# Loading K and V through a DRAM view with 32 KB rows, in an attention forward-and-backward kernel for one core

## The chip, the cores and the metric

One core of one Trainium2 chip. Times are device microseconds of that core.

PE is the engine of matrix products, DVE that of vectors, ACT that of activations. SP (SyncE) issues loads here and POOL (GpSimd) stores. A DMA moves data between DRAM and SBUF, the memory that the engines work on; 16 DMA engines do it. A descriptor is one run of bytes that a copy reads or writes in one piece, and a packet is one record of a DMA engine in the trace.

## The reference, cut to what matters

One token attends to a cache of 4,096 positions with 32 heads of 128, beside a small dense layer. The function returns the output and the gradients of all inputs.

```python
q = (x @ wq).reshape(B, Sq, H, Dh).transpose(0, 2, 1, 3)          # H = 32, Dh = 128
scores = einsum("bhqd,bhkd->bhqk", q, k_cache) * Dh ** -0.5       # Sk = 4096
p = softmax(scores)
o = einsum("bhqk,bhkd->bhqd", p, v_cache)
a = o.transpose(...).reshape(B, Sq, H * Dh) @ wo
# out = g * a + (1 - g) * b ; then the vjp: dK and dV are as large as K and V
```

K and V are 1 MB a head each and are read once. dK and dV are 1 MB a head each and are written once. That is 134 of the 165 MB that the kernel moves. The weights and their gradients are the rest.

## The kernel before

A tile of K has partition p holding positions 32p to 32p+31, so 8 KB in one run in each partition. In DRAM the runs of neighbouring partitions also follow each other: four partitions are 32 KB in one run. That is what the change wants to use.

```python
Kv = A_k_cache.rearrange("b h (p j) d -> (b h) p j d", p=P)     # P = 128, j = 32
Vv = A_v_cache.rearrange("b h (p j) d -> (b h) p j d", p=P)
# ... four buffers each of Kn and Vn, five of dV/dK, three of wo_g, four of the transposed tiles:
outs = ctx.enter_context(tc.tile_pool(name="outs", bufs=5))
tsb = ctx.enter_context(tc.tile_pool(name="tsb", bufs=4))

def load_k(h):
    if h < H:
        kts[h] = kv_in.tile([P, J, Dh], BF16, name="Kn", tag="Kn", bufs=KB)
        nc.sync.dma_start(kts[h][:], Kv[h])
# ... load_v the same with Vn and Vv
def load_wo(g):
    if g < NG:
        wos[g] = wts.tile([P, G, D], BF16, name="wo_g", tag="wo_g", bufs=3)
        nc.sync.dma_start(wos[g][:], wo_v[g])
# ... the main loop; all loads go through the one SP queue, in this order
for h in range(H):
    hh, g = h % G, h // G
    if hh == 3:
        load_wo(g + 2)          # waits until the store of dwo has left this wo_g buffer
        # ... load_wq every other time
    load_k(h + 3)
    load_v(h + 3)
    # ... steps of the projections
    period(h)                   # transposes, softmax, dP, dQ; dK and dV on VectorE
    # dK and dV are stored by nc.gpsimd.dma_start, the POOL queue
```

Of the kernel before, what the change touches and what calls it, by code (L numbers as in the profile page):

```python
# [16 lines left out]
def kernel(  # L17
# [24 lines left out]
    nc = tc.nc  # L42
    P = 128
# [18 lines left out]
    assert Dh == P and J % 8 == 0 and D % P == 0 and H % WG == 0  # L62
    assert 0 < FR <= P and FCN == 14

    Kv = A_k_cache.rearrange("b h (p j) d -> (b h) p j d", p=P)
    Vv = A_v_cache.rearrange("b h (p j) d -> (b h) p j d", p=P)
    dKv = out_2.rearrange("b h (p j) d -> (b h) p j d", p=P)
    dVv = out_3.rearrange("b h (p j) d -> (b h) p j d", p=P)
    wq_v = A_wq.rearrange("(rc r) c -> r rc c", r=P)
# [43 lines left out]
    kts, vts, wqs, wos = {}, {}, {}, {}  # L113

    def load_k(h):
        if h < H:
            kts[h] = kv_in.tile([P, J, Dh], BF16, name="Kn", tag="Kn", bufs=KB)
            nc.sync.dma_start(kts[h][:], Kv[h])

    def load_v(h):  # L120
        if h < H:
            vts[h] = kv_in.tile([P, J, Dh], BF16, name="Vn", tag="Vn", bufs=VB)
            nc.sync.dma_start(vts[h][:], Vv[h])

    def load_wq(w):
        if w < H // WG:
# [15 lines left out]
    load_wq(0)  # L142
    load_wo(0)
    load_k(0)
    load_v(0)
    load_k(1)
    load_v(1)
    load_wo(1)
    w1_sb = mlp.tile([P, RC, F], BF16, name="w1_sb", tag="w1_sb")
# [3 lines left out]
    nc.sync.dma_start(b1c[:, 0:FM], b1_v)  # L153
    nc.sync.dma_start(b1c[0:FR, FM:FCN], B_b1[FB:F].rearrange("(p c) -> p c", c=1))
    load_k(2)
    load_v(2)
    load_w2(0)
    w2r = mlp.tile([FR, D], BF16, name="w2r", tag="w2r")
# [688 lines left out]
```

## Time and profile before

| what | before |
|---|---|
| time, median of 3 runs | 413.23 us (413.08 to 413.69) |
| span of the profiled run | 411.8 us |
| SP load queue (q1), POOL store queue (q0), of 16 engines' span | 48.3%, 48.2% |
| DVE, PE, ACT busy | 74%, 72%, 43% |

These are lines of the page of before. The first two are the span in 40 equal slices: the busy tenths of the 16 DMA engines, and the GB/s they moved. The next two are the DMA queues: packets, MB, share of 16 engines' span. The last four are the DMA issues: how many, KB each, and the median us from issue to landing.

```profile
DMA  7999999999999999999999999999999999999990
GB/s 293 419 416 400 424 423 415 424 422 423 421 425 422 423 418 421 423 423 420 424 420 423 423 407 420 421 406 386 399 421 419 426 419 422 422 384 372 377 358 14
...
q1 hardware_dynamic: 14404, 82.03, 48.3%
q0 software_dynamic: 12240, 82.03, 48.2%
...
Kn<-in_A_k_cache_dram SPq DMA_DIRECT2D x32, 1024.0 KB, 23.9
Vn<-in_A_v_cache_dram SPq DMA_DIRECT2D x32, 1024.0 KB, 29.0
out_dram<-dV_sb POOLq DMA_DIRECT2D x32, 1024.0 KB, 11.8
out_dram<-dK_sb POOLq DMA_DIRECT2D x31, 1024.0 KB, 12.0
```

The digit is 9 from the second slice to the last but one, at 415 to 426 GB/s in most slices (29 of 40).

The chain that ended last, as the page of before has it (first by engine, then by line):

```profile
DMA 38%; DVE 33%; PE 19%; ACT 4%; issue 3%; POOL 0%; ACTq 0%; SPq 0%; POOLq 0%; DVEq 0%
DMA Kn<-in_A_k_cache_dram 30%; PE tr L586 8%; DVE dK_sb L611 7%; DVE dV_sb L611 7%; DMA out_dram<-dV_sb 6%; DVE junk L382 4%; ACT tT L588 3%; PE sA L655 3%; DVE junk L285 3%; PE sA L595 2%; PE sB L708 2%; DVE junk L534 1%; DVE junk L491 1%; DMA vec_rows<-in_gate_w_dram 1%; DVE dj L695 1%
```

Who waited for whom in before (us in total, times, longest), two lines of it:

```profile
PE tr L586 <- DMA Kn<-in_A_k_cache_dram: 6.5, 4, 2.3
...
DVE dK_sb L611 <- DMA out_dram<-dV_sb: 4.4, 1, 4.4
```

```profile
SPq L133 <- DMA out_dram<-wo_g: 54.1, 5, 14.1
```

Waiting for K is 30% of the chain, yet PE waits for it 6.5 us in all. The table by stretches shows where the DMA is not full. The last two columns are the DMA share and the GB/s, and a full DMA reads 1.01 or so:

```profile
core 0: us, PE busy (x) PEld busy (x) DVE busy (x) ACT busy (x) POOL busy (x), PEclk, DMA share, GB/s
220.00:260.00 40.00, 34.57 (x646) 31.53 (x647) 35.21 (x87) 23.00 (x51) 5.92 (x11) 0.93 1.01 417
360.00:370.00 10.00, 4.40 (x73) 3.84 (x69) 5.61 (x14) 3.07 (x7) 1.36 (x2) 0.94 0.95 396
370.00:380.00 10.00, 9.17 (x146) 8.64 (x145) 7.19 (x15) 4.09 (x9) 3.81 (x5) 0.72 0.89 359
380.00:390.00 10.00, 4.34 (x119) 3.57 (x117) 9.05 (x18) 1.79 (x6) 4.30 (x6) 0.79 0.94 376
360.00:390.00 30.00, 17.91 (x331) 16.05 (x327) 21.85 (x44) 8.95 (x21) 9.46 (x13) 0.82 0.93 377
```

### The profile page before, as it was taken

How to read it: one execution, taken by the hardware profiler on the slowest of the kernel's cores; microseconds unless marked ns; L12 is line 12 of the kernel's file. 1: busy time of each engine (PE TensorE's matmuls, PEld its weight loads, DVE VectorE, ACT ScalarE, POOL GpSimd, SP SyncE). 2: the span in 40 equal slices, each digit the busy share in tenths (PEclk: the TensorE clock that was granted, in tenths of full speed). 3: DMA queues.
4: the chain of work that ended last, by engine and by line, in shares of the span. 5: the costliest groups of instructions: out<-in, count | busy, mean ns of one | idle time of the engine just before them, and what ended most of it. 6: DMA issues, size and time to landing. Idle time of an engine off the chain costs nothing.

```text
span 411.8 us, 13602 instructions
## 1 busy us (share of the span) xinstructions
PE 296.3 (72%) x5872; PEld 268.2 (65%) x5872; DVE 303.1 (74%) x791; ACT 177.1 (43%) x411; POOL 50.8 (12%) x99
## 2 busy tenths in 40 slices
PE   0688898588887888188887888338887789949300
PEld 0578787587786777178877777338777778848200
DVE  3339666856899999377698898537999997957860
ACT  1355555254545555046542557215554455534000
POOL 0001111000111111011101112001111121113410
PEclk9999999889999999779996999758999999997755
DMA  7999999999999999999999999999999999999990
GB/s 293 419 416 400 424 423 415 424 422 423 421 425 422 423 418 421 423 423 420 424 420 423 423 407 420 421 406 386 399 421 419 426 419 422 422 384 372 377 358 14
DMA packets 26744, 164.93 MB, mean 401 GB/s; under 512 B 2956, under 2 KB 3020, under 8 KB 10428
## 3 DMA queue, kind: packets, MB, share of 16 engines
q1 hardware_dynamic: 14404, 82.03, 48.3%
q0 software_dynamic: 12240, 82.03, 48.2%
q8 instruction: 46, 0.75, 0.7%
q14 instruction: 14, 0.11, 0.1%
q10 hardware_dynamic: 40, 0.01, 0.0%
HBM read 82.03 MB, written 82.03 MB: 398 GB/s over the span
## 4 chain that ended last, share of the span: by engine, by line
DMA 38%; DVE 33%; PE 19%; ACT 4%; issue 3%; POOL 0%; ACTq 0%; SPq 0%; POOLq 0%; DVEq 0%
DMA Kn<-in_A_k_cache_dram 30%; PE tr L586 8%; DVE dK_sb L611 7%; DVE dV_sb L611 7%; DMA out_dram<-dV_sb 6%; DVE junk L382 4%; ACT tT L588 3%; PE sA L655 3%; DVE junk L285 3%; PE sA L595 2%; PE sB L708 2%; DVE junk L534 1%; DVE junk L491 1%; DMA vec_rows<-in_gate_w_dram 1%; DVE dj L695 1%
## 5 line engine op out<-in xcount | busy, mean ns | idle before, releaser
L588 ACT COPY tT<-tr 128x512 f32<-128x512 f32 x256 | 142.2, 587 | 129.7 <-PE tr L586 128.9
L595 PEld LDWEIGHTS <-tT 128*128 128x128 bf16 x2048 | 79.7, 98 | 44.4 <-ACT tT L588 34.5
L586 PE MATMUL tr<-ident_f,Kn 128*128 128x128 f32 x512 | 82.2, 299 | 6.5 <-DMA Kn<-in_A_k_cache_dram 6.5
L611 DVE TENSOR_TENSOR dK_sb<-ds_bf,qd 128x2048 bf16<-128x2048 bf16 x64 | 77.7, 1215 | 4.4 <-DMA out_dram<-dV_sb 4.4
L611 DVE TENSOR_TENSOR dV_sb<-p_bf,qd 128x2048 bf16<-128x2048 bf16 x64 | 77.9, 1218 | 0.2 <-issue 0.2
L586 PE MATMUL tr<-ident_f,Vn 128*128 128x128 f32 x512 | 72.5, 277 | 0.0
L586 PEld LDWEIGHTS tr<-ident_f,Kn 128*128 128x128 f32 x512 | 61.6, 153 | 7.7 <-issue 5.2
L595 PE MATMUL sA<-qd,tT 128*128 128x48 bf16 x1024 | 48.6, 187 | 23.7 <-ACT dq_all L713 12.8
L586 PEld LDWEIGHTS tr<-ident_f,Vn 128*128 128x128 f32 x512 | 55.9, 141 | 0.0
L595 PE MATMUL sB<-qd,tT 128*128 128x48 bf16 x1024 | 46.3, 183 | 0.0
L638 POOL DMA_DIRECT2D out_dram<-dV_sb x32 | 18.2, 569 | 170.2 <-DVE dV_sb L611 58.5
L655 PEld LDWEIGHTS <-Vn 128*128 128x128 bf16 x1024 | 30.6, 96 | 10.4 <-issue 10.4
L655 PE MATMUL sA<-e_bf,Vn 128*128 128x48 bf16 x1024 | 31.2, 184 | 7.6 <-DVE zs L675 6.2
L628 POOL DMA_DIRECT2D out_dram<-dK_sb x31 | 18.3, 591 | 145.3 <-DVE rz L677 97.2
L708 PE MATMUL sB<-ds_bf,Kn 128*128 128x48 bf16 x1024 | 31.5, 184 | 1.4 <-DVE ds_bf L697 1.4
L708 PEld LDWEIGHTS <-Kn 128*128 128x128 bf16 x1024 | 28.9, 97 | 1.6 <-issue 1.6
L659 DVE TENSOR_REDUCE m<-sA 128x1 f32<-128x32 f32 x32 | 6.0, 189 | 32.2 <-PE sA L595 25.6
L285 DVE SCALAR_TENSOR_TENSOR junk<-wo_g,da_bc 128x640 bf16<-128x640 bf16 x32 | 26.2, 820 | 1.7 <-ACT da_bc L226 1.1
L695 DVE TENSOR_SCALAR_CACHE_REDUCE dj<-sB,rz 128x128 f32<-128x128 f32 x32 | 11.1, 345 | 21.3 <-PE sB L689 21.3
L382 DVE SCALAR_TENSOR_TENSOR junk<-wq_g,dq_bc 128x1024 bf16<-128x1024 bf16 (+1 forms) x25 | 25.1, 1005 | 0.2
L275 PE MATMUL qc_ps<-cols_bf,wq_g 128*128 128x1 bf16 x160 | 5.3, 164 | 22.1 <-DMA wq_g<-in_A_wq_dram 22.1
L275 PEld LDWEIGHTS <-wq_g 128*128 128x128 bf16 x160 | 4.8, 100 | 22.6 <-DMA wq_g<-in_A_wq_dram 22.4
(154 smaller groups left out, 280.7 us busy)
## 6 DMA issues: line engine op xcount, KB each, us to landing
Kn<-in_A_k_cache_dram SPq DMA_DIRECT2D x32, 1024.0 KB, 23.9
Vn<-in_A_v_cache_dram SPq DMA_DIRECT2D x32, 1024.0 KB, 29.0
out_dram<-dV_sb POOLq DMA_DIRECT2D x32, 1024.0 KB, 11.8
out_dram<-dK_sb POOLq DMA_DIRECT2D x31, 1024.0 KB, 12.0
wq_g<-in_A_wq_dram SPq DMA_DIRECT2D x4, 1280.0 KB, 30.3
wo_g<-in_A_wo_dram SPq DMA_DIRECT2D x8, 640.0 KB, 7.4
out_dram<-wo_g POOLq DMA_DIRECT2D x8, 640.0 KB, 11.3
out_dram<-dwq_t POOLq DMA_DIRECT2D x5, 896.0 KB, 14.4
```

The lines of the kernel that those rows point to most:

```text
L275: nc.tensor.matmul(qc_ps[:, hh:hh + 1], lhsT=wq[:, rc, off + hh * Dh:off + (hh + 1) * Dh], rhs=x_bf[:, rc:rc + 1], start=(rc == 0), stop=( ...
L285: nc.vector.scalar_tensor_tensor(junk[:, 0:D], in0=wos[g][:, i, :], scalar=1.0, in1=da_bc[:], op0=ALU.mult, op1=ALU.mult, accum_out=gp["do ...
L382: nc.vector.scalar_tensor_tensor(junk[:, c0:c1], in0=wqs[w][:, rc, c0:c1], scalar=1.0, in1=dq_bc[:, w * WG * Dh + c0:w * WG * Dh + c1], op ...
L586: nc.tensor.transpose(tp[:, t, :], flat[:, k * P:(k + 1) * P], ident_f[:])
L588: nc.scalar.copy(sb[:].rearrange("p a b -> p (a b)"), tp[:].rearrange("p a b -> p (a b)"))
L595: nc.tensor.matmul(out[:, 2 * k:2 * k + W], lhsT=tb[:, t, par, :], rhs=vec[:, par, :].unsqueeze(1).to_broadcast([P, W // 2, 2]), start=(pa ...
L611: nc.vector.tensor_tensor(dst[:, a:b, :].rearrange("p j (a b) -> p j a b", b=2), col[:, a:b, :].unsqueeze(2).to_broadcast([P, n, Dh // 2, 2]),
L628: nc.gpsimd.dma_start(dKv[h], st["dK"][:])
L638: nc.gpsimd.dma_start(dVv[h], st["dV"][:])
L655: nc.tensor.matmul(O, lhsT=vts[h][:, j, :], rhs=st["e"][:, j:j + 1].to_broadcast([P, W]), start=(j == 0), stop=(j == J - 1))
L695: nc.vector.tensor_scalar(dj[:], PT, rz[:], None, ALU.mult, ALU.add, accum_out=dd[:])
L708: nc.tensor.matmul(DQ, lhsT=kts[h][:, j, :], rhs=ds[:, j, 0:1].to_broadcast([P, W]), start=(j == 0), stop=(j == J - 1))
```

## The change

Its intent: let one read descriptor cover the 32 KB of four partitions, so that a quarter as many packets carry K and V, while the writes into SBUF stay 8 KB each.

```diff
-    Kv = A_k_cache.rearrange("b h (p j) d -> (b h) p j d", p=P)
-    Vv = A_v_cache.rearrange("b h (p j) d -> (b h) p j d", p=P)
+    Kw = A_k_cache.rearrange("b h (c r) d -> (b h) c (r d)", c=P // 4)
+    Vw = A_v_cache.rearrange("b h (c r) d -> (b h) c (r d)", c=P // 4)
# ... in load_k and load_v
-            nc.sync.dma_start(kts[h][:], Kv[h])
+            nc.sync.dma_start(kts[h][:].rearrange("p j d -> p (j d)"), Kw[h])
-            nc.sync.dma_start(vts[h][:], Vv[h])
+            nc.sync.dma_start(vts[h][:].rearrange("p j d -> p (j d)"), Vw[h])
```

## The prediction

> **What bounds the kernel now.** The 16 DMA engines. The page's 40 slices show DMA busy at "9" from the second slice to the last but one, about 420 GB/s. The queue table gives the SP load queue 48.3% and the POOL store queue 48.2% of 16 engines' span, 82 MB each: with instruction fetch 97% of 411.8 us. No compute engine is near that (DVE 74%, PE 72%). In the chain of waits K loads are the largest entry (30%, four stretches of 27 to 34 us), yet the waits view has PE waiting for K only 6.5 us in all: progress, freeing of buffers and issue of loads go round together at the speed of the DMA. The table by stretches shows where the engines are not full: DMA share 0.79 in the first 10 us, 0.95, 0.89 and 0.94 in 360 to 390 us (1.01 to 1.02 when full), then a drain to about 401 us and 10 us of end work.
>
> **What the change does.** Bytes, issues, buffers and compute stay. The reads of K and V change: 8,192 descriptors of 8 KB become 2,048 of 32 KB, for 67 of the 165 MB moved. The 8 KB writes into SBUF stay. Two effects:
>
> 1. Cost per packet. The packet records fit a line: 2,048 B took 84 ns, 5,120 B 196, 8,192 B 309: 0.0366 ns per byte and 9 ns fixed.[...] If it goes with the read packet, 32 KB takes about 1,209 ns (estimate from that line) instead of 4 x 309 = 1,236: 27 ns times 128 packets per engine, 3.5 us. If the writes set it, nothing. I count half: 1.7 us, all critical, since the DMA is full.
>
> 2. Arbitration.[...] from about 50 to 70 us each queue gets half. With load packets four times as large, a backlogged load queue should get about four fifths. Loads then land much sooner (now 23.9 us for K, 29.0 for V, median), stores later (now 11.8) while loads are queued, and PE's waits for K turn into DVE waits for the five output buffers (4.4 us now). As the DMA is full either way, this moves work and saves little: the thin stretch at 360 to 390 us, about 2.5 us of idle DMA, fills, because the last loads land earlier and more stores are left. I count 1.5 us.
>
> **Prediction.** 413.2 - 3.2 = 410.0 us, within 404 to 417 (8 in 10). Faster by over 2% 0.10, within 2% 0.80, slower by over 2% 0.10.
>
> **What would show it.** Step 1: load packets of 32,768 B at about 1,209 ns, and some 6,100 packets fewer. Step 2: median K and V landing under 20 us, dV and dK landing longer, new DVE waits for stores at the outer products, DMA share in 360 to 390 us near 1.01. Unchanged: compute durations, bytes, DMA share about 97%.
>
> **What would make it wrong.**[...] If starved stores stop DVE, and through it PE, while the load queue has nothing to do, gaps appear in the DMA row. If the gaps I don't count (start, 250 to 300 us) also fill, 406 is possible.

The sum: 1.7 + 1.5 = 3.2 us. The 9 ns come from the line through the packet times of before, and that they go with the read, by half, was the guess. The four fifths are the estimate: in before two queues with packets of 8 KB share the bytes by halves (4.22 MB of loads, 4.18 of stores from 50 to 70 us); if packets four times as large came as often as those of the other queue, they would have four of five bytes. The trace of before does not show that; wide16, wide32 and both2 below test it.

## More of the kernel before

Executions of the kernel before all lay between 412.89 and 413.93 us (0.3%).

The dwo gradient is computed into its own wo_g buffer and stored from there, so this buffer comes free when the store has landed.

## The result, and the profile after

The changed kernel took 413.17 us (median of 4 runs, 412.91 to 413.59) against 413.27 us of before in the same rounds (413.08 to 413.69). The ratio is 0.9997, 95% interval 0.998 to 1.0015: the same. (A ratio is the mean time of one kernel's runs over that of the other's of the same rounds, so it is not quite the ratio of the medians.) Executions over 1.5% slower than the fastest of the same kernel are left out of the means.

The same lines of the page of after:

```profile
DMA  7999999999999999999999999999999999999980
GB/s 290 418 415 404 422 424 414 422 423 422 421 424 423 421 423 415 425 423 424 421 420 424 423 407 419 422 416 390 414 421 424 422 422 421 422 379 383 401 338 14
...
q1 hardware_dynamic: 14404, 82.03, 48.5%
q0 software_dynamic: 12240, 82.03, 48.1%
...
Kn<-in_A_k_cache_dram SPq DMA_DIRECT2D x32, 1024.0 KB, 23.3
Vn<-in_A_v_cache_dram SPq DMA_DIRECT2D x32, 1024.0 KB, 28.9
out_dram<-dV_sb POOLq DMA_DIRECT2D x32, 1024.0 KB, 11.6
out_dram<-dK_sb POOLq DMA_DIRECT2D x31, 1024.0 KB, 12.7
```

The packet counts are what they were, to the packet: 14,404 on the load queue. A quarter as many K and V packets would have left 8,260. Loads land after 23.3 and 28.9 us, as before, and stores after about 12 us. None of the signs that the prediction named is there.

The chain of after, and the waits that answer to those of before:

```profile
DVE 36%; DMA 33%; PE 17%; issue 6%; ACT 4%; POOL 1%; ACTq 0%; SPq 0%; POOLq 0%; DVEq 0%
DMA Kn<-in_A_k_cache_dram 23%; DVE dK_sb L611 9%; DVE dV_sb L611 8%; PE tr L586 7%; DMA out_dram<-dV_sb 6%; DVE junk L382 4%; ACT tT L588 3%; PE sA L655 3%; DMA out_dram<-wo_g 3%; DVE junk L285 3%; PE sA L595 2%; PE sB L708 2%; DVE junk L534 1%; DVE junk L491 1%; DMA vec_rows<-in_gate_w_dram 1%
```

```profile
PE tr L586 <- DMA Kn<-in_A_k_cache_dram: 6.1, 4, 2.2
...
DVE dK_sb L611 <- DMA out_dram<-dV_sb: 4.6, 1, 4.6
```

```profile
SPq L133 <- DMA out_dram<-wo_g: 53.6, 5, 13.5
```

K has 23% of the chain instead of 30%, while the waits are the same within half a us. The chain follows whichever of several near-equal waits came last, so its shares differ between two executions that do the same work. The stretches of after, with the columns of before (so too in all tables of stretches below):

```profile
220.00:260.00 40.00, 34.74 (x637) 31.73 (x638) 35.14 (x88) 22.57 (x51) 5.94 (x11) 0.92 1.01 418
360.00:370.00 10.00, 4.52 (x78) 4.08 (x79) 5.35 (x10) 2.94 (x8) 1.84 (x2) 0.83 0.89 374
370.00:380.00 10.00, 9.04 (x164) 8.31 (x162) 7.73 (x17) 5.00 (x11) 3.30 (x6) 0.83 0.96 389
380.00:390.00 10.00, 3.21 (x85) 2.50 (x80) 8.84 (x21) 0.54 (x3) 3.86 (x6) 0.68 1.00 400
```

The stretches near the end differ too: 0.89, 0.96, 1.00 instead of 0.95, 0.89, 0.94, and 0.95 instead of 0.93 over the 30 us. The program turned out to be the same (next paragraph), so this is the size of the difference between two executions. The prediction had read 1.5 us of gain from such lines.

**The program.** The two kernels were built and their instructions compared, field by field. Every instruction, wait and buffer is equal; only the recorded source text differs. This is the load of K for head 0, in both:

```
opcode DMACopy, queue qSPDynamicHW
read  in_A_k_cache_dram  [step 4096, count 128] [step 1, count 4096]   (elements of 2 bytes)
write Kn                 [step 4096, count 128] [step 1, count 4096]
```

As written in the changed kernel the read side is [step 16384, count 32] [step 1, count 16384]. In the finished program both sides have the shorter run, that of the write: the builder has turned 32 rows of 32 KB into 128 rows of 8 KB again. So the change never reached the chip. In the program of wide32 below, whose loads are issued by hand, 31 loads of K do have [step 16384, count 32].

### The profile page after: what moved, and what is told of

Same layout as the page of the kernel before. It is cut to its first block, busy times and chain, and to the rows that moved or that the text cites. A ratio compares the mean times of both kernels' runs of the same rounds, so it can differ in the third digit from the quotient of the medians.

```text
span 410.8 us, 13602 instructions
## 1 busy us (share of the span) xinstructions
PE 298.9 (73%) x5872; PEld 270.8 (66%) x5872; DVE 303.1 (74%) x791; ACT 177.3 (43%) x411; POOL 50.9 (12%) x99
## 3 DMA queue, kind: packets, MB, share of 16 engines
q1 hardware_dynamic: 14404, 82.03, 48.5%
## 4 chain that ended last, share of the span: by engine, by line
DVE 36%; DMA 33%; PE 17%; issue 6%; ACT 4%; POOL 1%; ACTq 0%; SPq 0%; POOLq 0%; DVEq 0%
DMA Kn<-in_A_k_cache_dram 23%; DVE dK_sb L611 9%; DVE dV_sb L611 8%; PE tr L586 7%; DMA out_dram<-dV_sb 6%; DVE junk L382 4%; ACT tT L588 3%; PE sA L655 3%; DMA out_dram<-wo_g 3%; DVE junk L285 3%; PE sA L595 2%; PE sB L708 2%; DVE junk L534 1%; DVE junk L491 1%; DMA vec_rows<-in_gate_w_dram 1%
## 5 line engine op out<-in xcount | busy, mean ns | idle before, releaser
L586 PE MATMUL tr<-ident_f,Kn 128*128 128x128 f32 x512 | 84.2, 304 | 6.1 <-DMA Kn<-in_A_k_cache_dram 6.1
L611 DVE TENSOR_TENSOR dK_sb<-ds_bf,qd 128x2048 bf16<-128x2048 bf16 x64 | 77.7, 1215 | 4.6 <-DMA out_dram<-dV_sb 4.6
L611 DVE TENSOR_TENSOR dV_sb<-p_bf,qd 128x2048 bf16<-128x2048 bf16 x64 | 78.0, 1218 | 0.3 <-issue 0.3
L586 PEld LDWEIGHTS tr<-ident_f,Kn 128*128 128x128 f32 x512 | 63.2, 156 | 7.3 <-issue 6.2
L638 POOL DMA_DIRECT2D out_dram<-dV_sb x32 | 18.3, 571 | 167.8 <-DVE dV_sb L611 57.1
L628 POOL DMA_DIRECT2D out_dram<-dK_sb x31 | 18.3, 592 | 146.1 <-DVE rz L677 96.8
L275 PE MATMUL qc_ps<-cols_bf,wq_g 128*128 128x1 bf16 x160 | 5.4, 164 | 19.8 <-DMA wq_g<-in_A_wq_dram 19.5
L275 PEld LDWEIGHTS <-wq_g 128*128 128x128 bf16 x160 | 4.9, 99 | 20.4 <-DMA wq_g<-in_A_wq_dram 19.8
## 6 DMA issues: line engine op xcount, KB each, us to landing
Kn<-in_A_k_cache_dram SPq DMA_DIRECT2D x32, 1024.0 KB, 23.3
Vn<-in_A_v_cache_dram SPq DMA_DIRECT2D x32, 1024.0 KB, 28.9
```

Of the source, the lines that this page charges most:

```text
L275: nc.tensor.matmul(qc_ps[:, hh:hh + 1], lhsT=wq[:, rc, off + hh * Dh:off + (hh + 1) * Dh], rhs=x_bf[:, rc:rc + 1], start=(rc == 0), stop=( ...
L586: nc.tensor.transpose(tp[:, t, :], flat[:, k * P:(k + 1) * P], ident_f[:])
L611: nc.vector.tensor_tensor(dst[:, a:b, :].rearrange("p j (a b) -> p j a b", b=2), col[:, a:b, :].unsqueeze(2).to_broadcast([P, n, Dh // 2, 2]),
L628: nc.gpsimd.dma_start(dKv[h], st["dK"][:])
L638: nc.gpsimd.dma_start(dVv[h], st["dV"][:])
```

## The experiments

Theory A: the change had no effect because the program is the same, and real 32 KB reads do what the prediction said of them (or something else, to be seen). Rival B: the chip did read 32 KB at a time, the records list only the 8 KB writes, and the size of a read matters to nothing. The comparison of the programs speaks for A. It does not show what a record of a wide read looks like, nor whether the prediction's two effects exist. For that the loads were issued by hand, so that the two sides stay in the program as written. All runs gave correct results.

| run | reads, writes of K and V | other edit | median us | before in the same rounds | ratio (95%) |
|---|---|---|---|---|---|
| plain8 | 8 KB, 8 KB | by hand | 413.51 | 413.32 | 1.0002 (0.999 to 1.0015) |
| wide32 | 32 KB, 8 KB | by hand | 415.55 | 413.32 | 1.0045 (1.0031 to 1.0058) |
| write2 | 8 KB, 2 KB | by hand | 421.57 | 413.32 | 1.0199 (1.0185 to 1.0213) |
| both2 | 2 KB, 2 KB | by hand | 425.73 | 413.32 | 1.0295 (1.0278 to 1.0311) |
| wide16 | 16 KB, 8 KB | by hand | 413.60 | 413.42 | 1.0006 (0.9993 to 1.0019) |
| plain_late | 8 KB, 8 KB | wo after K, V | 414.75 | 413.42 | 1.0039 (1.0026 to 1.0052) |
| wide32_late | 32 KB, 8 KB | wo after K, V | 415.77 | 413.42 | 1.0048 (1.0036 to 1.006) |
| wide16_late | 16 KB, 8 KB | wo after K, V | 414.50 | 413.42 | 1.0027 (1.0014 to 1.004) |
| tail32 | 32 KB from head 27 on | by hand | 413.68 | 413.33 | 1.0007 (0.9995 to 1.0019) |
| early32 | 32 KB in heads 1 to 26 | by hand | 414.98 | 413.33 | 1.0046 (1.0029 to 1.0063) |
| plain_wo4 | 8 KB, 8 KB | four wo_g buffers | 413.62 | 413.51 | 1.0002 (0.9988 to 1.0016) |
| wide32_wo4 | 32 KB, 8 KB | four wo_g buffers | 414.68 | 413.51 | 1.0029 (1.0016 to 1.0042) |

By a measure of 2%, only both2 is slower, write2 is unclear (its interval holds 1.02) and all others are the same as before. Below, "slower" is said where the interval of the ratio leaves out 1; most of these differences are half a per cent or less.

### plain8: the hand-built load, with nothing changed

Head 0 is loaded as before in all hand-built kernels: a first build without that did not compile.

```diff
+    def load_as(h, out, in_, out_p, in_p):
+        if h == 0:
+            nc.sync.dma_start(out_p, in_p)
+            return
+        src = copy.replace(nc.sync.lower_ap_dma(in_)[0], is_dma=False)
+        dst = copy.replace(nc.sync.lower_ap_dma(out)[0], is_dma=False)
+        nc.sync.add_instruction(mybir.InstDMACopy(
+            name=nc.get_next_instruction_name(), engine=mybir.EngineType.SP, ins=[src], outs=[dst],
+            mode="Copy", queue="qSPDynamicHW", cce_op=ALU.bypass))
+    Kw = A_k_cache.rearrange("b h (c r) d -> (b h) c (r d)", c=Sk * Dh * 2 // 8192)
# ... Vw the same
-            nc.sync.dma_start(kts[h][:], Kv[h])
+            load_as(h, kts[h][:].rearrange("p j d -> p (j d)"), Kw[h], kts[h][:], Kv[h])
# ... V the same
```

> Control: the K and V loads of heads 1 to 31 built by hand, 8 KB read and 8 KB write descriptors as before. Both theories: same time as before within 0.5% (412 to 415 us), 8,192 load packets of 8,192 B at 309 ns, K and V landing at 23 to 29 us. Only the SP issue of each load may get a few tenths of a us longer.

Measured: 413.51 us, ratio 1.0002, 8,192 packets of 8,192 B. The way the load is issued costs nothing that these runs resolve.

### wide32: reads of 32 KB, for real

```diff
-    Kw = A_k_cache.rearrange("b h (c r) d -> (b h) c (r d)", c=Sk * Dh * 2 // 8192)
+    Kw = A_k_cache.rearrange("b h (c r) d -> (b h) c (r d)", c=Sk * Dh * 2 // 32768)
```

> The read descriptors of heads 1 to 31 really are 32 KB, writes 8 KB. Theory A (the change never reached the program, since the builder matched the two sides to 8 KB again): this run differs in the trace from the change: about 1,984 load packets of 32,768 B in the records instead of 7,936 of 8,192 B, and the two effects of the prediction appear: 1,209 to 1,236 ns a packet, K and V landing under 20 us, new DVE waits for stores; time 408 to 413 us. Rival B (the change did issue 32 KB reads, but records list the 8 KB writes and the size of reads matters to nothing): trace and time as those of the change, 413 us, 8,192 B packets, K landing 23 us. Rival C:[...] packets well over 1,236 ns and over 417 us.

Measured: 415.55 us, ratio 1.0045. The ratio stands for 1.9 us more than before, the medians for 2.2; the profiled execution was the slowest of the five (416.66 us). Lines of its page, the load queue and the issues:

```profile
q1 hardware_dynamic: 8452, 82.03, 48.2%
...
Kn<-in_A_k_cache_dram SPq DMA_DIRECT2D x32, 1024.0 KB, 18.3
Vn<-in_A_v_cache_dram SPq DMA_DIRECT2D x32, 1024.0 KB, 19.5
out_dram<-dV_sb POOLq DMA_DIRECT2D x32, 1024.0 KB, 19.8
out_dram<-dK_sb POOLq DMA_DIRECT2D x31, 1024.0 KB, 19.4
```

The load queue has 8,452 packets, and the packet records list 1,984 of 32,768 B. So a record is a read, rival B falls, and the changed kernel, whose trace has none of these, did not read 32 KB at a time. Rival C, whose assumed cause is cut above as no run shows it, falls as well: the packets are not well over 1,236 ns (mean 1,241), and the time is not over 417 us.

The prediction's second effect is there: K and V land sooner (18.3 and 19.5 us instead of 23.9 and 29.0), stores later (19.8 and 19.4 instead of 11.8 and 12.0). The waits of DVE for output buffers grew from 4.4 to 21.2 us, and SP's wait for wo_g buffers from 54.1 to 87.6 us. (The helper moves the line numbers by 14: L625 is before's L611.)

```profile
DVE dV_sb L625 <- DMA out_dram<-dK_sb: 11.0, 3, 4.8
...
DVE dK_sb L625 <- DMA out_dram<-dV_sb: 10.2, 3, 8.1
```

```profile
SPq L147 <- DMA out_dram<-wo_g: 87.6, 5, 19.1
```

The stretches:

```profile
220.00:260.00 40.00, 31.69 (x609) 29.02 (x609) 34.90 (x87) 18.35 (x43) 5.36 (x10) 0.85 0.95 363
240.00:250.00 10.00, 8.30 (x165) 7.39 (x166) 9.60 (x25) 5.37 (x13) 1.07 (x2) 1.00 0.84 343
360.00:390.00 30.00, 21.93 (x453) 19.76 (x450) 26.23 (x56) 12.44 (x29) 8.38 (x11) 0.92 0.98 401
```

From 220 to 260 us the DMA share is 0.95 instead of 1.01, and 0.84 from 240 to 250 us. SP issues nothing between 233 and 250 us in this run: it stands at the load of wo, whose buffer waits for a starved store (15.3 us from issue to landing), and the loads of K and V stand behind it. From 360 to 390 us the share is up, 0.98 instead of 0.93, as the prediction had it. But the kernel is slower.

The packet records give the first effect (mean times of packets; "fastest" is the lowest 1%):

| run | K and V packet | forecast by the line | fastest | median | mean | sum of K and V, over 16 engines |
|---|---|---|---|---|---|---|
| before | 8,192 B | 309 | 309 | 309 | 312.4 | 160.0 us |
| wide16 | 16,384 B | 609 | 611 | 612 | 616.2 | 157.8 us |
| wide32 | 32,768 B | 1,209 | 1,213 | 1,231 | 1,241.2 | 158.9 us |
| wide32_wo4 | 32,768 B | 1,209 | 1,213 | 1,229 | 1,254.7 | 160.6 us |

The fastest packets nearly meet the line: 1,213 ns against 4 x 309 = 1,236, so 7.7 ns for each read saved. On average, 32 KB packets take longer than the line has it, for a reason that no run here shows. The sum of K and V is 2.2 us less than before in wide16, just what the line gives, 1.1 us less in wide32 and not less at all in wide32_wo4; the four runs with the reads and the order of loads of before (before, after, plain8, plain_wo4) have 159.9 to 160.1. In wide16 and wide32 the 2,048 B packets of the other loads grew, from a mean of 87.9 ns to 94.4 and 95.8 (87.9 to 89.8 in those four). The 5,120 B ones went from 204.2 to 214.0 in wide32, but to 215.3 in plain8 as well, so that is scatter. All packets together took 402.4 us over 16 engines in wide32, against 401.0 in before and 400.2 to 401.3 in those four. The saving of step 1 is real packet by packet, and neither this sum nor the time shows it. (The sum is not the time either: in both2 it grows by 20.6 us and the time by 12.4.)

### write2 and both2: where the fixed cost of a packet sits

```diff
# write2: reads 8 KB, writes 2 KB
+    Kw = A_k_cache.rearrange("b h (p s r) d -> (b h) p s (r d)", p=P, s=1)
+            load_as(h, kts[h][:].rearrange("p (s r) d -> p s (r d)", s=4), Kw[h], kts[h][:], Kv[h])
# both2: s=4 on both sides
```

(The reverse, reads of 2 KB and writes of 8 KB, did not compile.)

> Reads stay 8 KB, writes are 2 KB. If the fixed 9 ns goes with the read packet (prediction, step 1): load packets stay 8,192 B at 309 ns and the time stays at 413 us. If it goes with the write descriptor: four times 84 = 336 ns for 8 KB, 27 ns times 496 per engine, 13.4 us more, 427 us.

> Reads and writes both 2 KB. The line of packet times gives 84 ns per 2 KB, 336 ns for 8 KB instead of 309: 13.4 us more, about 427 us. Arbitration by packets: against 8 KB stores the loads get about a fifth while both queues are backlogged, so stores land sooner than the 11.8 us of before (under 9 us) and PE waits for K grow over 6.5 us. If engines share by bytes or time instead, landings stay near those of before plus a few per cent.

Measured: write2 421.57 us, neither 413 nor 427. Its load packets are still 8,192 B, with a mean of 323.8 ns instead of 312.4, so on average 3.8 ns for each of the three added writes; store packets grew from 314.4 to 319.9 ns as well. The fastest 1% still took 309 ns, so this is not a cost that every packet pays. But the time is 8.2 us longer: more writes cost time with the reads unchanged. That is why counting half of step 1 was not foolish; but the half that belongs to reads did not show up in the time when reads got larger.

both2 took 425.73 us, 12.4 us more than before (425.73 - 413.32), near the 13.4 expected. Of these, 8.2 came with the shorter writes (write2) and 4.2 more with the shorter reads (425.73 - 421.57). PE's waits for K grew to 22.9 us and stores landed after 8.8 us, as expected.

The shares of the two queues also come out near the forecast, but only in short slices. Over stretches of 5 us the median share of the load queue in the bytes of both2 is about 0.5, because bursts of stores alternate with loads alone. So the traces were cut into slices of 0.5 us, and those kept in which nearly all traffic of each queue (97%) was K and V, or dK and dV. In before, the load queue's share lies between 0.4 and 0.6 in 189 of 297 slices. With reads of 16 KB it lies between 0.6 and 0.8 in 173 of 302 (wide16), with 32 KB between 0.7 and 0.9 in 136 of 259 (wide32). With 2 KB it lies between 0.1 and 0.3 in 198 of 371, and over 0.8, where hardly a store is left, in 66. One record of each queue in turn would give 0.50, 0.67, 0.80 and 0.20. So in most of these slices the shares fit turns that go by records, whatever their size, and not by bytes, which would give 0.50 in all four. How many records make up one turn, no run here shows.

### plain_late and wide32_late: wo after K and V

```diff
     if hh == 3:
-        load_wo(g + 2)
# ...
     load_k(h + 3)
     load_v(h + 3)
+    if hh == 3:
+        load_wo(g + 2)
```

> Control, 8 KB reads: the load of wo for group g+2 is put after K and V of the same head on the SP queue instead of ahead of them. In before SP waits 54 us for the wo_g buffers, but its load queue does not run dry meanwhile, so both theories expect no gain: 412 to 414 us.

> Real 32 KB reads (415.6 us) with the same reordering. Theory A: the loss in wide32 is the SP queue held up by the wait for a wo_g buffer (87.6 us), whose store is starved, while K and V queue up behind it and the load queue runs dry (DMA share 0.78 to 0.89 at 240 to 250 us). Then that dip goes, and the time falls to 410 to 413 us. Rival B: the loss is DVE waiting for output buffers (21 us of waits for stores): then the dip stays and the time stays at 414.5 to 416.5 us. Rival C: the packets themselves are slower than the line gives (mean 1,241 ns instead of 1,209): then the dip goes but the time stays over 413.5 us.

Measured: plain_late 414.75 us, slower than before by 0.4%, which I had not expected: DVE now waits 32.4 us for the late wo itself. wide32_late 415.77 us. The dip from 240 to 250 us is gone (DMA share 1.03 instead of 0.84), and SP's waits for wo_g stores fell from 87.6 to 46.0 us, but the time did not fall. That is what rival C expected. But the edit costs something of its own, so the pair does not settle the question; against its control wide32_late is 1.0 us slower by the medians (415.77 - 414.75), and the two intervals overlap.

### wide16 and wide16_late: half the width

The edits are those of wide32 and wide32_late with 16384 in place of 32768.

> Reads of 16 KB. Split by packet size: while both queues are backlogged the loads get about two thirds or a little less (32 KB got about three quarters, 8 KB half). Landing of K and V between 19 and 28 us, of stores between 12 and 19 us. Time between before and wide32: 412 to 415 us; packets of 16,384 B at 609 to 620 ns.

> Reads of 16 KB with wo after K and V. Theory A: 410.5 to 413 us, at or under the control; rivals: no better than wide16.

Measured: wide16 413.60 us, the same as before (ratio 1.0006). Landing lies between: K 19.4, V 24.0, dV 17.1 us. DVE waits for stores 11.2 us. All packets together took 400.7 us over 16 engines against 401.0. The line would have saved 2.2 us here (one read in two, 9 ns, 248 packets per engine), and the packets of K and V alone did save that (157.8 against 160.0). wide16_late 414.50 us, no better than its control within 0.1%.

### tail32 and early32: the end and the rest apart

```diff
-        if h == 0:
+        if h < 27:                  # tail32
+        if h == 0 or h >= 27:       # early32
             nc.sync.dma_start(out_p, in_p)
```

The load of head 27 is issued when head 24 begins, after the last load of wo. So tail32 has what step 2 counted on, without the queue held up by wo.

> 32 KB reads only for the loads of heads 27 to 31, which are issued after the last load of wo, so that nothing on the SP queue waits for a starved store. Theory A (wide32 gains at the end what the prediction counted in step 2, and loses more in the middle): DMA share at 360 to 390 us over 0.96 on average instead of 0.93, no dip at 220 to 260 us, time 411.5 to 412.8 us. Rival B (wide reads bring nothing anywhere, the end included): 413.2 to 414.5 us.

> The complement: 32 KB reads for heads 1 to 26, 8 KB for the last five. Theory A: the loss without the gain: 415.5 to 417.5 us, DMA share at 360 to 390 us at 0.93 again, dips at 220 to 260 us as in wide32. Rival B: 415 us or less, the loss is shared out over both parts.

Measured: tail32 413.68 us, ratio 1.0007; no gain. early32 414.98 us, ratio 1.0046, the whole of wide32's loss. The stretches of tail32, then of early32:

```profile
220.00:260.00 40.00, 34.29 (x637) 31.37 (x638) 35.09 (x88) 22.52 (x51) 5.94 (x11) 0.92 1.01 417
360.00:390.00 30.00, 23.61 (x464) 21.43 (x464) 27.23 (x57) 13.32 (x30) 9.00 (x12) 0.90 0.85 345
```

```profile
220.00:260.00 40.00, 31.84 (x607) 29.24 (x607) 34.85 (x87) 18.22 (x43) 5.37 (x10) 0.85 0.93 362
360.00:390.00 30.00, 17.91 (x343) 16.02 (x340) 22.97 (x47) 9.45 (x22) 9.00 (x12) 0.82 0.99 408
```

In tail32 the DMA is less full at 360 to 390 us, 0.85 instead of 0.93 (0.93 to 0.95 in before, after, plain8 and plain_wo4). In early32, whose last loads are plain, it is fuller, 0.99. This is the reverse of the argument of step 2. The last load of V lands at 355.3 us in tail32, at 369.6 in before. After it only stores remain, and these come no faster than the compute engines make them: DVE is busy 27.2 of those 30 us in tail32, 21.9 in before. Where the DMA of tail32 is thinnest, from 366 to 370 us (0.53), DVE is busy for 3.96 of the 4 us. That one queue could not fill the engines is ruled out: with stores alone the share is 0.99 from 390 to 400 us. The fuller end of wide32 and early32 goes with a kernel that runs late, not with a gain; plain_late, with reads of 8 KB, is slower too and has 1.01 there. Theory A of these two runs, that the end gains and the middle loses more, falls in its first half. Rival B has the right ranges for both times, but the loss is not shared out: tail32 has none of it.

### plain_wo4 and wide32_wo4: a fourth wo_g buffer

```diff
-    tsb = ctx.enter_context(tc.tile_pool(name="tsb", bufs=4))
+    tsb = ctx.enter_context(tc.tile_pool(name="tsb", bufs=3))
# ... in both tiles with tag wo_g (load_wo and dwq_l)
-    tag="wo_g", bufs=3
+    tag="wo_g", bufs=4
```

With four tsb tiles as well the kernel did not build: the pool mlp wanted 34 KB in each partition of SBUF, and 32.2 KB were left, by the builder's message.

> Control, 8 KB reads: four wo_g buffers instead of three (and three transpose tiles instead of four, to make room). SP no longer waits for the store of a wo_g buffer (54 us in before), yet the load queue was never dry through it: 412.5 to 414 us.

> 32 KB reads with the fourth wo_g buffer, K and V in the old order. Theory A (the loss of 1.7 to 2.2 us in wide32 and early32 is SP held by the wait for a wo_g buffer): the 87.6 us of SP waits for wo_g stores and the dip at 220 to 260 us go (DMA share 1.00 or more there), and the time comes to within 0.2% of the control, 412.5 to 414.2 us. Rival B (the loss is DVE held by starved stores): the dip or others like it stay, 414.6 to 416.5 us. In neither do I still expect the 410 us that was predicted, since tail32 brought no gain at the end.

Measured: plain_wo4 413.62 us, the same as before. wide32_wo4 414.68 us, ratio 1.0029. Its waits of DVE for stores, and the stretch of the dip:

```profile
DVE dV_sb L625 <- DMA out_dram<-dK_sb: 24.0, 5, 8.8
...
DVE dK_sb L625 <- DMA out_dram<-dV_sb: 7.7, 2, 6.6
```

```profile
220.00:260.00 40.00, 33.54 (x667) 30.25 (x665) 38.72 (x98) 21.91 (x50) 5.36 (x10) 0.96 1.01 413
```

SP's waits for wo_g stores are gone from its list, and so is most of the dip: 1.01 from 220 to 260 us (0.94 from 240 to 250 us, where wide32 had 0.84). The time is 1.1 us over the control (414.68 - 413.62) where wide32 was 1.9 to 2.2 over before. The two intervals overlap, so that the wo wait makes up some of the loss fits the runs and is not proven. What is left goes with DVE's waits for stores, 31.7 us now, and with packet times that sum to 402.6 us over 16 engines against 401.0 of the control. Which of these two sets the remaining 1.1 us stays open. The result lies in the range that rival B gave, over that of theory A.

No version beat before. The best of the wide ones, wide16 and tail32, are within noise of it.

## Why the prediction was right or wrong

- **What bounds the kernel: right.** The DMA engines (the two queues take 96.5% of their span, DVE is busy for 74%). Where packets were made dearer, the time grew: both2 added 12.4 us, write2 8.2.
- **The step that failed: "8,192 descriptors of 8 KB become 2,048 of 32 KB".** The builder gave both sides of these copies runs of 8 KB, so the program has 8,192 of 8 KB as before. The runs showed the same 14,404 load packets, and wide32 shows what the record would have been. Nothing was removed, so nothing was gained: 413.17 us instead of 410.0. The range, 404 to 417, held the time; the gain of 3.2 us that it was built around did not exist. The list of what would make it wrong did not contain this case.
- **Step 1, "I count half: 1.7 us, all critical": not borne out even by real wide reads.** The fastest packets nearly met the line, 1,213 ns against 1,209. The sum of K and V packets fell by 2.2 us in wide16 and 1.1 in wide32, and rose by 0.7 against its control in wide32_wo4 (160.6 - 159.9), but the time fell in none. The fit to the most common packet times gave what a packet of 32 KB can cost (1,209 ns, 1,213 for the fastest), not what it cost on average in wide32 (1,241), nor was what K and V saved there saved in the whole (402.4 us for all packets, 401.0 in before).
- **Step 2, the shares and landings: right, though not for this change.** With real 32 KB reads the loads' share rose to 0.7 to 0.9 in most slices (the prediction said about four fifths), with 2 KB reads it fell to 0.1 to 0.3. K and V landed under 20 us with 32 KB reads (18.3 and 19.5), stores later (19.8 and 19.4), and DVE waited 21.2 us for stores. In the change nothing of it happened.
- **Step 2, "the thin stretch [...] fills, because the last loads land earlier [...] I count 1.5 us": wrong.** tail32 made the loads land earlier and the stretch grew thinner. There DVE was the busy one (27.2 of 30 us): the stores came as fast as dK, dV and the gradients of the weights were made.
- **"If starved stores stop DVE [...] gaps appear in the DMA row": happened** in wide32 and early32, by a route that was not named: the load of wo that waited for a starved store held all loads behind it on the SP queue (in wide32 none was issued from 233 to 250 us, and the DMA share fell to 0.84 from 240 to 250 us).
- **Chances.** "Within 2%" had 0.80 and came true, for another reason than the one given.

## What to carry to other kernels

Before costing a change of an access pattern, find out whether it is still in the program after building: here a view that was wider on one side of the copy alone was cut back to the other side's rows (32 rows of 32 KB to 128 of 8 KB, 14,404 load packets with and without the change). After a run, compare packet sizes and counts first; if they are equal to the packet, look at the program before looking for a mechanism. Where the DMA is full, as here, larger reads on one queue bought their earlier landing from the other queue (wide32: K after 18.3 us instead of 23.9, dV after 19.8 instead of 11.8), so ask which buffers the delayed transfers keep occupied, and what stands behind them. A fuller DMA row near the end can go with a slower kernel: 0.99 from 360 to 390 us in early32 (414.98 us), 0.93 in before (413.33 us in the same rounds).
